# One more score block turned by DMA, with another table of steps, in a two-layer attention and token-mixer kernel

## The chip, the cores and the metric

The kernel runs on one core of a Trainium2 chip. The metric is the device time in microseconds of one execution, as the median of several. Before the change it is 765.40 us (three runs, 765.38 to 765.44). The core has TensorE (PE, with its weight loads shown as PEld), VectorE (DVE), ScalarE (ACT), GpSimd (POOL) and SyncE (SP), which here issues nearly all DMAs in one queue.

## The reference

There are two layers on 8 batches of 3200 rows. The first is an attention with a squared ReLU; its scores are z times its own transpose, so they are symmetric. The second mixes the tokens with weights that come from x itself.

```python
scores = (1.0 / S) * np.matmul(z, z.transpose(0, 2, 1))      # z: [8, 3200, 64]
attn = np.maximum(scores, 0.0) ** 2
x = u * np.matmul(attn, v)                                    # u, v: [8, 3200, 256]
wq, wk = x @ w_q, x @ w_k                                     # [8, 3200, 64]
W_tok = (1.0 / np.sqrt(64)) * np.einsum('bsd,btd->bst', wq, wk)
mixed = np.einsum('bst,btd->bsd', W_tok, x)
out = np.maximum(mixed, 0.0) @ w_out                          # w_out: [256, 256]
```

## The kernel before

**Tiles.** The 3200 rows of a batch are 25 row tiles of 128. As columns they make seven groups: groups 0 to 5 are 512 wide (four row tiles each), group 6 is 128 wide (one row tile). A score tile is one row tile against one group: 128 x 512, made by one matmul with 64 rows of contraction, so two of them run as a pair on the lower and the upper half of the array (`scores`, L296). The pair is emptied from PSUM into `g` by DVE or ACT with the ReLU (`first_stage`, L316 to L324), then squared by POOL or ACT into an fp16 tile `at` (`second_stage`, L326, L332 and L330). PSUM has three tiles for all of this (`pps`), and there are eleven `at` tiles.

**Turned blocks.** Scores are symmetric and so are their squares. A square whose block (gi, gj) is "turned" (`is_turned`, L237) is made once in group gi's columns, and a DMA transpose on SP's queue (L351) writes its mirror image into a home `tt`, from where it serves group gj. Block (gi, gj) means row group gj in group gi's columns. With `FAR = 2`, the blocks (0,1), (0,2), (1,2), (1,3), (2,3), (2,4), (3,4), (3,5), (4,5) are turned, and (0,4) besides: ten a batch, each of four score tiles, and two transposes each. There are seven homes (L285 to L294), given out by when the block in them was last read. Narrow mirror images for group 6 (`ts`) are turned as well.

**The second product.** For each group, x's 512 rows are the sum over all 25 row tiles of the transposed squares times v (`second_product`, L464). Its items are matmuls of 256 columns into two PSUM banks. Each is split into two with 64 rows of contraction, which run side by side: in the first pass the lower half works on one bank and the upper half on the other, then the lanes change banks (`swap_after`, L443) for the second pass. At the end of a group `gate` (L488) multiplies by u (DVE reads one bank at L507; ACT copies the other at L506 and POOL multiplies at L509). In the seventh group of a batch the two lanes keep one bank each (`is_split`).

**The second layer.** `turn_x` (L512) transposes x by DMA into one of four tiles. A "key block" (`keys_and_heads`, L813) projects x to queries and keys on TensorE, transposes the keys by DMA, and sums keys times x of the group before. When a batch is through, `mix` (L652) and `mix_out` (L678, on ACT) make the mixed rows for two groups at a time, and `project` (L804) multiplies a group of them by w_out, scales it on ACT (L739) and stores it.

**Steps.** The loop at L1028 runs in steps k = 3 to 167. A step scores up to six tiles (four if it holds a mix), empties them, squares those of the step before, and consumes, for the current group, tiles made two steps earlier (`LAG`) and turned tiles. How many steps a group gets follows from how many tiles are ready. A step may hold one key block, or one projection, or one mix, with or without a projection. Rules decide which (`key_due`, `mix_due`), except at the steps in the table `chosen` (L911), where letters say it: k, m, p. `heading_more` moves one score pair out of the head of a step. Loads, casts and transposes for the next batch are due a fixed number of steps after a batch began (`group_begun`, L866). After the loop a written order (`ENDING`) does what is left, with exactly three output groups still to be projected (`fillers`, L1237 and L1248).

Of the kernel before, what the change touches and what calls it, by code (L numbers as in the profile page):

```python
# [16 lines left out]
def kernel(  # L17
# [25 lines left out]
    FAR = 2  # L43
# [27 lines left out]
    def ps_tile(name):  # L71
        return pps.tile([P, 2, W], FP32, tag="ps", name=name)
# [162 lines left out]
    LASTG = NG - 1  # L235

    def is_turned(gi, gj):  # L237
        return gi < gj < LASTG and (gj <= gi + FAR or (gi, gj) == (0, 4))

# [2 lines left out]
    def group_of(ti):  # L244
        return max(gi for gi in range(NG) if starts[gi] <= ti * P)
# [8 lines left out]
    for b in range(B):  # L254
        for gi in range(NG):
            near = [t for t in range(NT) if is_turned(gi, group_of(t))]
            own = [
                t for t in range(NT) if t not in near and not is_turned(group_of(t), gi)
            ]
            if gi == LASTG:  # L260
                own = [t for t in own if group_of(t) not in FOR_SMALL]
            if b == 0 and gi == 0:
                order = [t for n0, nn in ZCH for t in range(n0, n0 + nn)]
                assert sorted(order) == sorted(near + own)
            else:
                odd = len(tiles) % 2
                order, rest = own[:odd], own[odd:]
                n_, m_ = len(near) // 2, (len(rest) + 1) // 2
                at_ = sorted(
                    [((i + 0.5) / max(n_, 1), near[2 * i : 2 * i + 2]) for i in range(n_)]  # L270
                    + [((i + 0.7) / max(m_, 1), rest[2 * i : 2 * i + 2]) for i in range(m_)]
                )
                for _, two in at_:
                    order = order + two
                if rest and len(rest) % 2:
                    order.remove(rest[-1])
                    order.append(rest[-1])
            many = W // widths[gi]
            tiles += [(b, gi, order[i : i + many]) for i in range(0, len(order), many)]
            ends[b, gi] = len(tiles)  # L280
# [5 lines left out]
    for b, gi, tis in tiles:  # L286
        gj = group_of(tis[0])
        if is_turned(gi, gj) and (b, gi, gj) not in tt_of:
            lefts = [t for t in range(NT) if is_turned(group_of(t), gj)]
            last_read = lefts.index(starts[gi] // P + 3) + 1  # L290
            tt_free.sort()
            tt_of[b, gi, gj] = tt_free[0][1]
            tt_free[0] = (b * NG + gj + last_read / len(lefts), tt_of[b, gi, gj])
# [79 lines left out]
    def whole(banks):  # L373
        return [
            lambda i=i: i.emit(ALL, i.start, i.stop) for bank in banks for i in bank
        ]
# [317 lines left out]
    def proj_items(b, gi, banks, half):  # L694
        js = range(2 * half, min(2 * half + 2, widths[gi] // P))
        return [
            Item(
                out=banks[half][:, ds((j % 2) * D, D)],
                lhsT=lambda r, dc=dc, j=j: rts[b, gi][r, dc, ts(j, P)],
                rhs=lambda r, dc=dc: wo[r, dc, :],  # L700
                start=(dc == 0 and j == js[0]),
                stop=(dc == ND - 1 and j == js[-1]),
            )
            for dc in range(ND)
            for j in js
        ]
# [14 lines left out]
    def proj_out(b, gi, src, ways):  # L721

        n0 = starts[gi] // P
        if groups:
            fo = pfo.tile([P, 2, W], FP32, tag="fo", name="fo")
        else:
            fo = pg.tile([P, 2, W], FP32, tag="g", name="fo")
        flat_out = fo[:].rearrange("p a w -> p (a w)")
        at = 0
        for on_dve, queue, n in ways:  # L730
            sl = slice(at * D, (at + n) * D)
            part = src[at // 2][:, 0 : n * D] if isinstance(src, list) else src[:, sl]
            if on_dve:
                nc.vector.tensor_scalar(
                    out=flat_out[:, sl], in0=part, scalar1=FINAL_SCALE, scalar2=None,
                    op0=AOP.mult,
                )
            else:
                nc.scalar.mul(out=flat_out[:, sl], in_=part, mul=FINAL_SCALE)  # L739
            queue.dma_start(  # L740
                out=rows(out, b)[:, n0 + at : n0 + at + n, :],
                in_=flat_out[:, sl].rearrange("p (n d) -> p n d", d=D),
            )
            at += n
# [41 lines left out]
    fillers = []  # L786
    to_load = []
    todo_mix, todo_proj, todo_between, at_phase, side = [], [], [], {}, []
# [15 lines left out]
    def project(b, gi):  # L804

        ps = ps_tile("fo")
        banks = [ps[:, 0, :], ps[:, 1, :]]
        src = ps[:].rearrange("p a w -> p (a w)")
        return [proj_items(b, gi, banks, half) for half in range(2)], lambda: proj_out(
            b, gi, src, [(False, nc.sync, widths[gi] // P)]  # L810
        )
# [54 lines left out]
    def group_begun(k, b, gi):  # L866
# [40 lines left out]

    heading_more = {165: -1}  # L910
    chosen = {  # L911
        18: "k", 19: "p", 20: "p", 21: "m", 35: "k", 36: "p", 38: "p", 101: "p", 142: "mp",
        147: "k", 148: "m", 149: "m", 159: "mp", 161: "p", 163: "m"
    }

    def mix_due(k):
# [104 lines left out]
    produced, consumed, k = 16, 6, 3  # L1021
# [6 lines left out]
    while groups:  # L1028
# [71 lines left out]
        b, gi = groups[0]  # L1100
# [134 lines left out]

    assert not at_phase and not side and not todo_between 
    fillers = todo_proj + fillers  # L1237
    assert not todo_mix and len(fillers) <= 3

    def acc_banks(name):  # L1240
        return [acc_tile(half, f"{name}{half}")[:] for half in range(2)]
# [112 lines left out]
```

## Time and profile before

| | |
|---|---|
| median of 3 runs | 765.40 us |
| the profiled execution | 765.49 us |
| its span, first to last instruction | 763.7 us |
| granted TensorE clock | 0.998 |
| TensorE busy | 754.3 us |
| ScalarE, GpSimd, VectorE busy | 551.1, 537.1, 461.9 us |
| busy share of the DMA queue of SP | 91.2% of 16 engines |
| HBM read, written | 59.38 MB, 26.21 MB |

All times are those of one profiled execution. A group's row names the line, the engine, the operation, what is written from what, the count, then the busy time, the mean of one in ns, and the idle time of the engine just before such instructions with what ended it. The chain is followed back from the last instruction: at each step to what released it. A matmul's duration is its latency; since matmuls overlap, the chain's pieces are the better measure of what a stretch costs. The DMA share adds up the times of packets, also of those that wait beside each other, so it can pass 1.

### The profile page before, as it was taken

How to read it: one execution, taken by the hardware profiler on the slowest of the kernel's cores; microseconds unless marked ns; L12 is line 12 of the kernel's file. 1: busy time of each engine (PE TensorE's matmuls, PEld its weight loads, DVE VectorE, ACT ScalarE, POOL GpSimd, SP SyncE). 2: the span in 40 equal slices, each digit the busy share in tenths (PEclk: the TensorE clock that was granted, in tenths of full speed). 3: DMA queues.
4: the chain of work that ended last, by engine and by line, in shares of the span. 5: the costliest groups of instructions: out<-in, count | busy, mean ns of one | idle time of the engine just before them, and what ended most of it. 6: DMA issues, size and time to landing. Idle time of an engine off the chain costs nothing.

```text
span 763.7 us, 29059 instructions
## 1 busy us (share of the span) xinstructions
PE 754.3 (99%) x12888; PEld 618.0 (81%) x12888; DVE 461.9 (60%) x458; ACT 551.1 (72%) x651; POOL 537.1 (70%) x351
## 2 busy tenths in 40 slices
PE   9999999999999999999999999999999999999996
PEld 6777888888888887888888888888878888888884
DVE  7655676546755567555665557656566565755534
ACT  8666776677767777687776877759777697776555
POOL 7897797768766678676787668866688665854540
PEclk9999999999999999999999999999999999999999
DMA  8999789887999969997899998999899999798636
GB/s 178 189 197 219 187 187 192 174 181 160 206 196 233 219 166 185 221 235 195 214 177 219 243 195 181 158 228 265 135 223 189 228 250 156 161 222 193 176 74 262
DMA packets 289614, 150.23 MB, mean 197 GB/s; under 512 B 265168, under 2 KB 268752, under 8 KB 289488
## 3 DMA queue, kind: packets, MB, share of 16 engines
q1 hardware_dynamic: 288768, 146.48, 91.2%
q0 software_dynamic: 576, 1.64, 1.1%
q8 instruction: 100, 1.64, 0.9%
q14 instruction: 26, 0.21, 0.1%
q10 hardware_dynamic: 144, 0.26, 0.1%
HBM read 59.38 MB, written 26.21 MB: 112 GB/s over the span
## 4 chain that ended last, share of the span: by engine, by line
PE 97%; DVE 2%; issue 0%; DMA 0%; ACT 0%; DVEq 0%; ACTq 0%
PE acc L369 72%; PE sc L307 12%; PE fo L369 5%; PE qk L369 5%; PE mx L657 1%; DVE x_sb L507 1%; DVE fo L1312 0%; DVE g L321 0%; PE ztp L130 0%; DMA z<-in_z_dram 0%; PE qk L610 0%; DVE zT L136 0%; PE xtx L634 0%; PE hd L644 0%; ACT fo L1316 0%
## 5 line engine op out<-in xcount | busy, mean ns | idle before, releaser
L321 DVE TENSOR_SCALAR g<-sc 128x1024 f32<-128x1024 f32 x329 | 400.5, 1223 | 240.5 <-PE sc L307 225.9
L332 POOL TENSOR_TENSOR at<-g 128x1024 f16<-128x1024 f32 x229 | 431.4, 1893 | 131.1 <-DVE g L321 106.5
L369 PE MATMUL acc<-v_sb,at 64*128 64x256 f16 (+1 forms) x7187 | 461.8, 269 | 1.6 <-DVE x_sb L507 0.5
L369 PEld LDWEIGHTS <-at 64*128 64x128 f16 (+1 forms) x7187 | 353.9, 94 | 86.9 <-PE acc L369 25.4
L330 ACT ACTIVATE at<-g 128x1024 f16<-128x1024 f32 x227 | 236.1, 1056 | 14.3 <-DVE g L321 7.2
L369 PE MATMUL acc<-v_sb,tt 64*128 64x256 f16 x2552 | 178.7, 269 | 0.0
L307 PE MATMUL sc<-zT 64*128 64x512 f16 (+1 forms) x1008 | 165.3, 357 | 0.2
L319 ACT ACTIVATE g<-sc 128x1024 f32<-128x1024 f32 x127 | 130.0, 1024 | 45.5 <-PE sc L307 43.2
L369 PEld LDWEIGHTS <-tt 64*128 64x128 f16 x2552 | 130.1, 94 | 14.2
L509 POOL TENSOR_TENSOR x_sb<-gt,u_sb 128x512 f16<-128x512 f32 x48 | 61.2, 1276 | 66.2 <-ACT gt L506 61.8
L678 ACT ACTIVATE rt<-mx 128x1024 f16<-128x1024 f32 x47 | 47.9, 1024 | 32.6 <-PE mx L657 32.5
L506 ACT COPY gt<-acc 128x512 f32<-128x512 f32 x48 | 28.0, 584 | 46.5 <-PE acc L369 44.7
L307 PEld LDWEIGHTS <-zT 64*128 64x128 f16 x1008 | 51.9, 94 | 8.8 <-issue 1.7
L369 PE MATMUL fo<-wo,rt 64*128 64x256 f16 (+1 forms) x696 | 57.9, 270 | 0.0
L544 ACT CAST qk<-qk 128x512 f16<-128x512 f32 x47 | 27.5, 585 | 34.3 <-PE qk L369 31.6
L369 PEld LDWEIGHTS <-rt 64*128 64x128 f16 (+1 forms) x696 | 35.5, 94 | 15.3 <-PE fo L369 6.3
L507 DVE TENSOR_TENSOR x_sb<-acc,u_sb 128x512 f16<-128x512 f32 x48 | 33.2, 691 | 20.3 <-PE acc L369 19.5
L739 ACT ACTIVATE fo<-fo 128x1024 f32<-128x1024 f32 x39 | 39.9, 1024 | 1.9 <-PE fo L369 1.7
L369 PEld LDWEIGHTS <-x_sb 64*128 64x128 f16 x672 | 29.8, 95 | 4.5 <-PE qk L369 0.9
L369 PE MATMUL qk<-kx,x_sb 64*128 64x64 f16 x672 | 32.8, 190 | 0.0
L369 PE MATMUL qk<-xT_sb,wkq 64*128 64x512 f16 (+3 forms) x118 | 25.8, 326 | 0.0
L369 PE MATMUL qk<-xT_sb,wqk 64*128 64x384 f16 (+3 forms) x148 | 24.8, 296 | 0.0
(86 smaller groups left out, 275.2 us busy)
## 6 DMA issues: line engine op xcount, KB each, us to landing
u_sb<-in_u_dram SPq DMA_DIRECT2D x48, 512.0 KB, 5.5
out_dram<-fo SPq DMA_DIRECT2D x43, 512.0 KB, 4.1
piece<-in_v_dram SPq DMA_DIRECT2D x42, 512.0 KB, 5.2
piece<-in_z_dram SPq DMA_DIRECT2D x7, 512.0 KB, 5.2
tt<-at SPq DMA_TRANSPOSE x162, 4.6
out_dram<-fo SPq DMA_DIRECT2D x9, 256.0 KB, 2.9
piece<-in_z_dram SPq DMA_DIRECT2D x7, 288.0 KB, 4.9
u_sb<-in_u_dram SPq DMA_DIRECT2D x8, 128.0 KB, 4.2
```

Source lines behind the costliest of these rows:

```text
L307: nc.tensor.matmul(out=sc[:, h, at : at + w], lhsT=zT[b][half : half + dqk, ds(z_at(b, h) + ti * P, P)], rhs=zT[b][half : half + dqk, ds(z ...
L319: nc.scalar.activation(out=g[:], in_=sc[:], func=RELU, scale=GSCALE)
L321: nc.vector.tensor_scalar(out=g[:], in0=sc[:], scalar1=0.0, scalar2=GSCALE, op0=AOP.max, op1=AOP.mult)
L330: nc.scalar.square(out=out, in_=g[:])
L332: nc.gpsimd.tensor_mul(out=out, in0=g[:], in1=g[:])
L369: return nc.tensor.matmul(out=self.out, lhsT=self.lhsT(rows), rhs=self.rhs(rows), start=start, stop=stop)
L506: nc.scalar.copy(out=upper[:], in_=accs[1][:])
L507: nc.vector.tensor_mul(out=x[:, 0:n], in0=accs[0][:, 0:n], in1=ug[:, 0:n])
L509: nc.gpsimd.tensor_mul(out=x[:, n : 2 * n], in0=upper[:], in1=ug[:, n : 2 * n])
L544: nc.scalar.copy(out=qks[b, gi][:, 0:gw], in_=out)
L678: nc.scalar.activation(out=out, in_=ps[:], func=RELU)
L739: nc.scalar.mul(out=flat_out[:, sl], in_=part, mul=FINAL_SCALE)
```

## The change

Row group 5 in group 2's columns becomes a turned block too: block (2,5). Its four tiles are squared in group 2 as before, and two more DMA transposes a batch write the mirror image for group 5. Group 5 computes 13 row tiles instead of 17 and reads 12 turned ones instead of 8. The number of score tiles falls from 912 to 880, and that of the steps by five (k = 3 to 162). The table of hand-chosen steps is another, since the steps have moved. The homes are the same seven, and they are given out anew by the same rule. In the last batch, the mixes that are left when scoring is over are three instead of two, and four output groups instead of three are left after the loop; the new lines project the first of them there, before the written ending.

```diff
     def is_turned(gi, gj):
-        return gi < gj < LASTG and (gj <= gi + FAR or (gi, gj) == (0, 4))
+        return gi < gj < LASTG and (gj <= gi + FAR or (gi, gj) in ((0, 4), (2, 5)))
...
-    heading_more = {165: -1}
+    heading_more = {64: -1}
     chosen = {
-        18: "k", 19: "p", 20: "p", 21: "m", 35: "k", 36: "p", 38: "p", 101: "p", 142: "mp",
-        147: "k", 148: "m", 149: "m", 159: "mp", 161: "p", 163: "m"
+        16: "m", 40: "k", 41: "p", 59: "", 139: "p", 140: "m", 141: "m", 142: "p", 143: "m",
+        145: "p"
     }
...
     fillers = todo_proj + fillers
-    assert not todo_mix and len(fillers) <= 3
+    assert not todo_mix
+    while len(fillers) > 3:
+        made_now, done_now = project(*fillers.pop(0))
+        for fn in whole(made_now):
+            fn()
+        done_now()
```

## The prediction

> **What bounds the kernel now.** I read the page's shares and chain first, then eight equal stretches of the span, then the chain inside single steps. The page:
>
> ```profile
> span 763.7 us, 29059 instructions
> PE 754.3 (99%) x12888; PEld 618.0 (81%) x12888; DVE 461.9 (60%) x458; ACT 551.1 (72%) x651; POOL 537.1 (70%) x351
> PE 97%; DVE 2%; issue 0%; DMA 0%; ACT 0%; DVEq 0%; ACTq 0%
> L321 DVE TENSOR_SCALAR g<-sc 128x1024 f32<-128x1024 f32 x329 | 400.5, 1223 | 240.5 <-PE sc L307 225.9
> L332 POOL TENSOR_TENSOR at<-g 128x1024 f16<-128x1024 f32 x229 | 431.4, 1893 | 131.1 <-DVE g L321 106.5
> L369 PE MATMUL acc<-v_sb,at 64*128 64x256 f16 (+1 forms) x7187 | 461.8, 269 | 1.6 <-DVE x_sb L507 0.5
> L330 ACT ACTIVATE at<-g 128x1024 f16<-128x1024 f32 x227 | 236.1, 1056 | 14.3 <-DVE g L321 7.2
> L319 ACT ACTIVATE g<-sc 128x1024 f32<-128x1024 f32 x127 | 130.0, 1024 | 45.5 <-PE sc L307 43.2
> ```
>
> TensorE is the chain (97%), and the 7187 product matmuls idled before them for 1.6 us in all. The other engines wait for it: DVE stood 225.9 us until a score matmul ended. By stretches (us, busy time of PE, PEld, DVE, ACT, POOL, then clock, DMA share, GB/s):
>
> ```profile
> 95.50:190.90 95.40, 95.13 (x1671) 79.33 (x1667) 57.69 (x58) 68.92 (x83) 75.32 (x48) 1.00 0.86 179
> 477.30:572.80 95.50, 95.37 (x1680) 78.54 (x1678) 58.88 (x57) 70.88 (x84) 69.81 (x44) 1.00 1.00 202
> ```
>
> PE leaves 0.13 us of 95.5 idle at full clock, so time is matmul columns. The DMA share stands at 1.00, which makes DMA the second thing to watch. It is a sum over packets and no saturation: a single step shows 1.24 and PE stays whole there (3.29 of 3.29):
>
> ```profile
> 102.17:105.46 3.29, 3.29 (x58) 2.55 (x54) 2.38 (x3) 2.65 (x3) 3.29 (x3) 1.00 1.24 269
> ```
>
> The chain inside a plain step (start, us, what) gives the prices:
>
> ```profile
> 99.04 0.43 PE sc L307 x4
> 99.48 1.31 PE acc L369 x24
> 100.79 0.22 PE sc L307 x2
> 101.00 1.33 PE acc L369 x24
> ```
>
> Two score matmuls run side by side on the two halves of the array, so a pair of them is 0.43/2 = 0.215 us, and 24 product matmuls take 1.31 us. The step is nothing else.
>
> **The change, part by part.**
>
> *Scores.* Block (2,5) gets its transpose from a DMA, so block (5,2) is no longer computed: 4 tiles a batch, 32 in all, 880 - 32 = 848 wide score matmuls, 16 pairs. 16 x 0.215 = 3.4 us leave the chain. The Trainium skill (TensorE: Matmul & The Clock Gate, Back-to-back issue gap) gives about 131 ns a matmul of 512 columns in a stream; 32 of them would be an estimated 4.2 us, and the sum below would end 0.8 us lower. The trace disagrees (0.43 us for four), because two share the array.
>
> *Evictions and squares.* 16 pairs fewer: by the built order DVE 329 to 318 and ACT 127 to 122 first stages, POOL 229 to 219 and ACT 227 to 221 squares. 11 x 1.223 = 13.5 us of DVE, 10 x 1.893 = 18.9 us of POOL, 5 x 1.024 + 6 x 1.056 = 11.5 us of ACT. These lie beside PE and are worth 0.
>
> *Steps.* The step loop runs to 162 instead of 167, since six tiles are scored a step and group 5 now takes two steps, not three. The product's items stay 5000. The two lanes change banks 232 instead of 239 times. What such a change costs:
>
> ```profile
> PEld L369 <- PE acc L369: 25.4, 106, 0.3
> ```
>
> A weight load waits 25.4/106 = 0.24 us there, but in the plain step above the score pair of 100.79 stands in the gap and the pass after it takes 1.33 against 1.31. So between 0.02 and 0.24 each, 0.1 to 1.7 us for seven; I take 0.2, by the step, which is PE itself.
>
> *Group starts.* At a group's start PE needs the accumulators that DVE and ACT are reading, and runs scores meanwhile. With a projection or a key block in the step the wait is covered; without one it isn't:
>
> ```profile
> 163.50 0.66 PE sc L307 x12
> 164.17 2.28 PE acc L369 x36
> 166.49 2.14 PE acc L369 x35
> ...
> 212.12 0.46 PE fo L369 x8
> 212.58 1.97 PE acc L369 x36
> 214.76 1.99 PE acc L369 x35
> ...
> 181.41 0.65 PE sc L307 x6
> 182.06 1.64 PE acc L369 x28
> 183.75 1.70 PE acc L369 x27
> ...
> 163.57 0.69 DVE L507 TENSOR_TENSOR x_sb<-acc,u_sb 128x512 f16<-128x512 f32 x1 [1.37 <-PE acc L369]
> ```
>
> At 163.50 three score pairs (0.66) are shorter than the DVE read that ends at 163.57 + 0.69 = 164.26, and the two passes take (2.28 - 1.97) + (2.14 - 1.99) = 0.46 us more than those at 212.58, which a projection covers. After the narrow seventh group (181.41) it is 1.64 + 1.70 against 55/24 x 1.31 = 3.00, so 0.3. By the step tables the start is bare at steps 7, 10, 37 (wide) and 41, 104 (narrow) before; after, at 7, 10, 16, 34, 44 (wide) and 141 (narrow, a mix and two score pairs). Net 2 x 0.46 - 0.3 = +0.6 us.
>
> *Moved key blocks and mixes.* Steps 79, 99 (a key block) and 140 (a mix) now share the step of a seventh group, which held a projection or nothing before. No row shows it: at best it covers the start as a projection does (0), at worst it costs a bare start, 0.46 each. I take 0, as the key block is the same kind of TensorE work as the projection.
>
> *The end.* Three mixes instead of two are flushed when scoring is over (step 160), and one output group, (6, 2), is projected after the loop. The matmul columns are the same. Each flushed mix is emptied by ACT:
>
> ```profile
> L678 ACT ACTIVATE rt<-mx 128x1024 f16<-128x1024 f32 x47 | 47.9, 1024 | 32.6 <-PE mx L657 32.5
> ...
> ACT G L1269 <- PE xtx L634: 3.9, 1, 3.9
> ```
>
> With three PSUM tiles the third mix needs one that a score eviction has left; the last pair is emitted half a step earlier, so 0, at worst one ACT row, 1.0 us. The later scaling of (6, 2), 1.0 us on ACT, falls into the 3.9 us that ACT stands before G: 0. Without that cover G would start up to 1.0 later. I take 0.1 for both.
>
> *DMA.* 16 more transposes, two a batch, go on SP's queue while group 2's columns are made; nothing leaves that queue. On SP and to landing:
>
> ```profile
> L351 SPq DMA_TRANSPOSE tt<-at x162: 1195/1373/4432, 13.1 to 719.6; - x162
> DMA to landing us min/median/max: 2.5/4.6/9.7
> SPq L351 <- POOL at L332: 45.9, 34, 3.0
> ACT at L330 <- DMA tt<-at: 4.8, 2, 3.2
> POOL at L332 <- DMA out_dram<-fo: 2.3, 1, 2.3
> ```
>
> 16 x 1.373 = 22 us of SP. Behind them in the queue stand x's transposes, the key transposes, u, the next batch's v and z, and the stores. The seven homes of turned blocks now hold eleven blocks a batch, not ten: by the tables a home is written in the very step of its last reader three times (steps 50, 91, 110) and in the step after it 17 times (twice before), and the transpose of x for (1, 5), asked for in step 39, waits for the key block of step 40, which frees the fourth of its tiles. Each holds SP for up to a step. The first reader of a turned block comes no sooner than two steps after its writing, as before. So PE need not notice: between 0 and the 4.8 + 2.3 us that ACT and POOL lost to DMAs in this trace. I take 0.2, near the low end, because PE lost nothing to those two.
>
> *Sum.* -3.4 - 0.2 + 0.6 + 0.1 + 0.2 = -2.7 us. The profiled execution took 765.49 us (span 763.7), 0.09 over the median of 765.40: 762.8 profiled, 762.7 as a median. Ends: -3.4 - 1.7 gives 760.4; the upper ends 0.6 + 1.4 + 1.0 + 7.1 on -3.5 give +6.6, 772.
>
> **The rivals.** (a) *The gain is eaten at the starts.* Key blocks and mix on the seventh group's steps cost a bare start each (3 x 0.46) and the third mix its 1.0: 762.7 + 2.4 = 765.1, no change. For it: the bare starts show that PE has no reserve at a group's start. Against: with a projection in that step the seventh group runs in this trace without a named wait.
>
> (b) *Slower: late transposes hold the `at` buffers.* Eleven at buffers feed PE; a square may not overwrite one whose transpose has not read it. The row "ACT at <- DMA tt" shows it twice, up to 3.2 us. In a plain step ACT has 3.29 us for a PSUM tile whose eviction takes 1.024, so some 2.3 us can be lost before PE waits. One wait of 3.2 a batch would cost 0.9 x 8 = 7.2: 769.9. It decides when PE loses over 2.7 + 1.5 = 4.2 us, 0.5 a batch. For: DMA share near 1.00 all through the middle, homes with no step to spare. Against: two such waits in 763.7 us now, and fewer squares.
>
> (c) *SP's issue is the bound.* If the sequencer that issues the DMAs set the pace, each of the 16 would lengthen the run: +22 us, 787. SP waits 45.9 us for POOL's squares alone, so it has time over. That a track solid with DMA issues is itself a bound is a rule of the Trainium skill (Perfetto Trace Analysis, What "DMA-bound" means); by that rule this trace is not there.
>
> **How the numbers follow.** Forecast 762.7, own range 761.0 to 763.8: 0.55. (a) 0.22. (b) 0.20. (c) 0.03. A measurement tells about 0.2%, 1.5 us, from no change: below 763.9 faster 0.55, up to 766.9 same 0.22, above it slower 0.23. The range reaches from 761.0 up to 767.5, where (a) and the weak cases of (b) lie; beyond it I leave 0.14, below it 0.04.
>
> **What the profile after would show.** Scores: 976 rows of L307 instead of 1008, its share of the chain down by 0.4 points. Starts: passes of 2.2 to 2.3 us for 36 matmuls at steps 16, 34, 44. DMA: tt<-at +16, landing times longer in the middle, more SP waits for PE. (a) shows as PE idle before acc at the seventh groups and at the flush. (b) shows as "ACT at" or "POOL at" waiting for DMA tt<-at many times, and then PE idle before sc. I am wrong if PE's idle time before L307 and L369, 1.8 us together with the next row, grows by more than 4 us.
>
> ```profile
> L307 PE MATMUL sc<-zT 64*128 64x512 f16 (+1 forms) x1008 | 165.3, 357 | 0.2
> ```

## The result and the profile after

The changed kernel takes 770.87 us as a median (767.31 to 773.31), the kernel before beside it 765.42 (765.38 to 765.76). The ratio is 1.0065, with a 95% interval from 1.0046 to 1.0084: slower by 0.65%, where 762.7 us had been forecast. The profiled execution of the changed kernel, 767.31 us, is the fastest of its four, so its trace shows the least of the loss. The four lie 6 us apart; those of the kernel before lie 0.4 us apart here, and 0.8 to 5.2 us in the larger sets further down.

The page of the changed kernel, the lines that answer to those shown of before:

```profile
span 765.4 us, 28908 instructions
PE 751.6 (98%) x12820; PEld 618.5 (81%) x12820; DVE 446.9 (58%) x447; ACT 541.7 (71%) x641; POOL 517.7 (68%) x340
q1 hardware_dynamic: 305664, 150.67, 95.3%
PE 92%; DMA 2%; DVE 2%; ACT 1%; issue 1%; POOL 0%; ACTq 0%; DVEq 0%; POOLq 0%
L332 POOL TENSOR_TENSOR at<-g 128x1024 f16<-128x1024 f32 x219 | 412.3, 1894 | 126.0 <-DVE g L321 71.9
L369 PE MATMUL acc<-v_sb,at 64*128 64x256 f16 (+1 forms) x6931 | 448.8, 269 | 2.3 <-DMA v_sb<-in_v_dram 0.9
L330 ACT ACTIVATE at<-g 128x1024 f16<-128x1024 f32 x221 | 229.4, 1055 | 36.0 <-DMA tt<-at 23.0
L307 PE MATMUL sc<-zT 64*128 64x512 f16 (+1 forms) x976 | 160.5, 356 | 1.0 <-ACT g L319 0.6
L369 PE MATMUL qk<-kx,x_sb 64*128 64x64 f16 x672 | 32.8, 190 | 1.1 <-DMA kx<-qk 1.1
```

TensorE has less work and is the chain for 92% of the span instead of 97%. DMAs, 0% before, now carry 2% of it. ACT's idle time before its squares has grown from 14.3 to 36.0 us, and most of it (23.0) ends with the landing of `tt`. The waits of the changed kernel (us in all, times, longest) say the same of POOL:

```profile
POOL at L332 <- DMA tt<-at: 28.3, 11, 3.7
ACT at L330 <- DMA tt<-at: 23.0, 9, 4.9
POOL v_sb L151 <- DMA piece<-in_v_dram: 8.1, 4, 4.1
```

Before, ACT's row was 4.8 us in two waits, and the two others did not exist. Two of the 95 us stretches, with the columns of the prediction's windows:

```profile
477.30:572.80 95.50, 95.37 (x1688) 78.95 (x1686) 56.57 (x57) 69.17 (x83) 66.68 (x42) 1.00 1.01 215
572.80:668.20 95.40, 94.10 (x1670) 78.40 (x1668) 57.01 (x56) 71.28 (x84) 65.48 (x42) 1.00 1.07 209
```

One of them is as whole as before (0.13 us idle), the next has lost 1.3 us. The loss sits at single places.

**What is late.** The landing time of `tt` has hardly moved (median 4.7 us, 4.6 before). It is the issue that comes late. The DMA queue of SP in the changed kernel (start, us, what):

```profile
152.53 1.35 SPq L351 DMA_TRANSPOSE tt<-at  x1
153.97 1.22 SPq L351 DMA_TRANSPOSE ts<-at  x1
155.28 1.20 SPq L551 DMA_TRANSPOSE kx<-qk  x1
156.57 1.18 SPq L551 DMA_TRANSPOSE kx<-ql  x1
157.80 0.57 SPq L195 DMA_DIRECT2D u_sb<-in_u_dram  x1
158.47 2.15 SPq L351 DMA_TRANSPOSE tt<-at  x1
```

There is no room between them. The key transpose at 156.57 belongs to step 32, whose first matmul stands at 137.20:

```profile
137.20 0.59 PE L307 MATMUL sc<-zT 64*128 64x512 f16 x4
```

So it is issued 19.4 us after its step began. SP issues in the order in which the code asks, so this lateness (issue of a DMA less the first matmul of the step that asks for it) can be worked out for each DMA of the step loop. It counts from the step's start, so a DMA that the step asks for late has some us even in an idle queue; what tells is the comparison. Its median, 90th percentile and largest value are 6.0, 9.5 and 12.4 us before, and 8.2, 13.9 and 19.4 after. The longest stretch in which SP issues one DMA right behind another (under 0.3 us between them) grows from 67 us (47 DMAs) to 82 us (58 DMAs, from 94 us on).

**Where TensorE waits.** A step's loss is its length less what its matmuls cost at the rate of the plain step. The sum of the losses has grown by 5.1 us, and 3.4 us of scores are gone; the difference is the 1.7 us by which the spans differ. Of the 5.1 us, 0.6 stand in the opening (in this profile alone; two later ones of the same kernel do not have them), 1.0 in the ending, and most of the rest at steps 16, 18, 95 and 146. At step 146 the chain names the DMA:

```profile
658.72 4.25 DMA kx<-qk
662.97 0.05 issue
663.02 0.52 PE qk L369 x10
```

Step 146 multiplies x by the keys of step 144, whose transpose was issued at 658.72, two short steps earlier. Ahead of steps 16, 18 and 95 the path is the one of rival (b). ACT before step 95, which begins at 425.85:

```profile
421.97 1.06 ACT L330 ACTIVATE at<-g 128x1024 f16<-128x1024 f32 x1 [3.01 <-DMA tt<-at]
...
425.81 1.00 ACT L319 ACTIVATE g<-sc 128x1024 f32<-128x1024 f32 x1
```

A square waits 3.01 us for its `at` buffer, what stands behind it on ACT is late, the eviction at 425.81 too, and TensorE, which needs that PSUM tile, loses 1.0 us.

### The profile page after: what moved, and what is told of

Its sections match the earlier page's. It is cut to its first block, busy times and chain, and to the rows that moved or that the text cites. A ratio compares the mean times of both kernels' runs of the same rounds, so it can differ in the third digit from the quotient of the medians.

```text
span 765.4 us, 28908 instructions
## 1 busy us (share of the span) xinstructions
PE 751.6 (98%) x12820; PEld 618.5 (81%) x12820; DVE 446.9 (58%) x447; ACT 541.7 (71%) x641; POOL 517.7 (68%) x340
## 4 chain that ended last, share of the span: by engine, by line
PE 92%; DMA 2%; DVE 2%; ACT 1%; issue 1%; POOL 0%; ACTq 0%; DVEq 0%; POOLq 0%
PE acc L369 69%; PE sc L307 11%; PE fo L369 5%; PE qk L369 5%; PE mx L657 1%; DVE g L321 1%; DMA v_sb<-in_v_dram 1%; DMA tt<-at 1%; DMA kx<-qk 1%; DVE x_sb L507 1%; ACT g L319 0%; DVE fo L1317 0%; ACT at L330 0%; ACT zT L188 0%; POOL at L332 0%
## 5 line engine op out<-in xcount | busy, mean ns | idle before, releaser
L321 DVE TENSOR_SCALAR g<-sc 128x1024 f32<-128x1024 f32 x318 | 386.5, 1223 | 238.9 <-PE sc L307 232.8
L332 POOL TENSOR_TENSOR at<-g 128x1024 f16<-128x1024 f32 x219 | 412.3, 1894 | 126.0 <-DVE g L321 71.9
L369 PE MATMUL acc<-v_sb,at 64*128 64x256 f16 (+1 forms) x6931 | 448.8, 269 | 2.3 <-DMA v_sb<-in_v_dram 0.9
L369 PEld LDWEIGHTS <-at 64*128 64x128 f16 (+1 forms) x6931 | 345.0, 94 | 82.6 <-PE acc L369 24.5
L330 ACT ACTIVATE at<-g 128x1024 f16<-128x1024 f32 x221 | 229.4, 1055 | 36.0 <-DMA tt<-at 23.0
L369 PE MATMUL acc<-v_sb,tt 64*128 64x256 f16 (+1 forms) x2776 | 189.1, 269 | 0.0
L307 PE MATMUL sc<-zT 64*128 64x512 f16 (+1 forms) x976 | 160.5, 356 | 1.0 <-ACT g L319 0.6
L369 PEld LDWEIGHTS <-tt 64*128 64x128 f16 (+1 forms) x2776 | 140.9, 94 | 15.3
L319 ACT ACTIVATE g<-sc 128x1024 f32<-128x1024 f32 x122 | 124.6, 1021 | 34.9 <-PE sc L307 33.5
L151 POOL CAST v_sb<-piece 128x1024 f16<-128x1024 f32 (+1 forms) x23 | 22.6, 981 | 8.1 <-DMA piece<-in_v_dram 8.1
```

The costliest lines, as they stand in the source:

```text
L307: nc.tensor.matmul(out=sc[:, h, at : at + w], lhsT=zT[b][half : half + dqk, ds(z_at(b, h) + ti * P, P)], rhs=zT[b][half : half + dqk, ds(z ...
L319: nc.scalar.activation(out=g[:], in_=sc[:], func=RELU, scale=GSCALE)
L321: nc.vector.tensor_scalar(out=g[:], in0=sc[:], scalar1=0.0, scalar2=GSCALE, op0=AOP.max, op1=AOP.mult)
L330: nc.scalar.square(out=out, in_=g[:])
L332: nc.gpsimd.tensor_mul(out=out, in0=g[:], in1=g[:])
L369: return nc.tensor.matmul(out=self.out, lhsT=self.lhsT(rows), rhs=self.rhs(rows), start=start, stop=stop)
```

## The experiments

Three theories were put to test. **Q**: SP's queue falls behind through its time for issuing, and what waits for it reaches TensorE. **D**: the transfers of the 16 transposes are the cost, through the DMA engines. **T**: the step table (bare starts, moved key blocks and mixes) is the cost. Medians are in us; each is to be read beside the kernel before in the same set of runs, which took 765.4 to 765.9.

### The 16 transposes taken out

Block (2,4)'s home is kept until group 5 has read it, too.

```diff
...
+            if (gi, gj) == (2, 5):
+                turned[b, gi, gj] = turned[b, 2, 4]
+                continue
```

> The changed kernel without the 16 transposes of block (2,5): block (5,2) reads the turned block (2,4) in its place, so the output of that block is left out. TensorE's work and the step table are those of the changed kernel, SP issues as many transposes as before. If the loss comes from the added transposes on SP's queue (theory Q) or from DMA traffic (theory D), the gain of the scores is seen: 762.5 to 764.0 us, and the longest time that an issue on SP comes after its step's start falls back from 19.4 to about 12.5 us. If the loss comes from the new step table, the bare starts and the moved key blocks and mixes (theory T), it stays at 769 to 771.

Measured 764.41 (763.62 to 766.22), ratio 0.9984 (0.9972 to 0.9997); lateness 11.3 us at the 90th percentile, 17.3 at most where about 12.5 had been expected. So part of the scores' gain is there, the transposes eat it and more, and T is not the main cause. But only 1.4 us are gained (1.9 in the profiled execution, 0.5 of them after the last matmul), not 2.9. The losses up to the last matmul tell where: 1.9 us more than before, of which 1.0 stands in the ending. The chain there in the kernel before:

```profile
744.02 0.44 PE fo L369 x4
744.46 0.44 PE hd L369 x4
```

and in this run:

```profile
740.65 0.89 PE fo L378 x8
741.54 0.02 issue
741.56 0.02 ACTq L748
741.58 0.04 issue
741.62 1.03 ACT fo L748
742.65 0.04 issue
742.69 0.60 PE hd L378 x4
```

The scaling of the output group that is now projected after the loop (1.03 us on ACT) stands on the chain, since `hd` needs the PSUM tile that it empties. The other 0.9 us are the bare starts at steps 16, 34 and 44 (0.64 to 0.69 lost in each, lane change included) and step 150, less those that went.

### The same transposes in the kernel before

```diff
...
-            if is_turned(gi, gj) or (gj == LASTG and gi in FOR_SMALL):
+            if is_turned(gi, gj) or (gi, gj) == (2, 5) or (gj == LASTG and gi in FOR_SMALL):
```

The homes are given out as in the changed kernel.

> The kernel before, with its step table and all its scores, plus the 16 transposes of block (2,5), which nothing reads; the block takes its home among the seven as long as in the changed kernel. Theory Q: the loss without the gain, 765.4 plus up to 8 us: 768 to 774, POOL and ACT waiting for DMA tt<-at for 20 us and more. Theory D: the same sign. Theory T: 765.2 to 766.0.

Measured 766.07 (764.89 to 769.53), ratio 1.001 (0.9999 to 1.0022), a miss for Q and D: nearly no loss, though SP is as late as in the changed kernel (13.6 at the 90th percentile) and POOL and ACT wait 33.8 and 12.3 us for `tt`. So the transposes cost little in the table of steps of before. That TensorE has less reserve against them in the changed kernel's shorter table fits this, and a later run with the transposes unread (below), but what in the table takes the reserve was not tested.

### Stores moved to ACT's queue

```diff
-            b, gi, src, [(False, nc.sync, widths[gi] // P)]
+            b, gi, src, [(False, nc.scalar, widths[gi] // P)]
```

> The changed kernel with the 45 or so stores of the step loop issued from ACT's queue instead of SP's; about 0.56 us each, some 25 us, leave SP, as much as the transposes of (2,5) added, and the DMA traffic is the same. Theory Q (SP's in-order queue falls behind): 762.5 to 764.5 us. Theory D (the transfers themselves, a DMA share of 1.01 to 1.07): no change, 769 to 771. Theory T (step table): no change, 769 to 771, or more, as ACT carries the issues.

> The kernel before with the same stores on ACT's queue, the control. Theory Q: SP was not the limit before, 765.0 to 765.8. If ACT's issue work costs PE anything by itself, it shows here: over 766.

Measured 780.91 with the change and 775.19 without it, where 763 and 765 had been expected of Q. The control shows why this says nothing on Q. ACT's timeline in the kernel before with that edit:

```profile
414.19 1.02 ACT L739 ACTIVATE fo<-fo 128x1024 f32<-128x1024 f32 x1
418.40 0.34 ACTq L740 DMA_DIRECT2D out_dram<-fo  x1
418.85 1.06 ACT L330 ACTIVATE at<-g 128x1024 f16<-128x1024 f32 x1 [3.63 <-DMA tt<-at]
```

The store stood for 3.2 us before it was issued. In the trace all DMAs of SP and ACT share eight completion semaphores in turn, and the store's was that of a transpose which SP had issued late:

```profile
412.75 1.24 SPq L351 DMA_TRANSPOSE tt<-at  x1
```

That one landed 5.6 us later, at 418.33, when ACT went on. So SP's lateness was passed on to ACT.

### The changed kernel again, and with the transposes unread

> The changed kernel once more, beside the three others on the same chip: 769 to 772 us if its loss of 5.4 us is its own and not that of one chip. Theory Q (SP's in-order queue falls behind, and what waits for it on POOL, ACT and PE stands at places that change from execution to execution) expects a spread of several us, and in the profile of a slower execution PE's idle time at more steps than 16, 95 and 146.

In the next kernel block (5,2) reads block (2,4)'s mirror image, and that of (2,5) is made for nobody; the homes are given out to suit:

```diff
...
-        return turned[b, gj, gi][rows, j, ti - starts[gj] // P, :]
+        read = 4 if (gj, gi) == (2, 5) else gi
+        return turned[b, gj, read][rows, j, ti - starts[gj] // P, :]
```

> The changed kernel with all its transposes, of which those of block (2,5) are read by nothing: block (5,2) reads the turned block (2,4), and the home of (2,5) comes free soon after its writing. The output of that block is left out. Theory Q: the 16 transposes cost the same whether they are read or not, 769 to 771 us, as the changed kernel. Theory H (the reads hold the homes and the homes hold SP): as without the transposes, 764 to 765.5.

Measured 771.95 (766.91 to 776.62), ratio 1.0088 (1.006 to 1.0117), for the first, and 766.88 (765.03 to 772.65), ratio 1.003 (1.0014 to 1.0046), for the second. The loss is the change's own. With the unread transposes the kernel is 1.5 us above the kernel before of its set, without them it was 1.4 below: they cost some 3 us, the read ones more. Neither Q's 769 to 771 nor H's 764 to 765.5 was met. Homes that hold SP (theory H) are not the reason: where SP is more than 6 us late, it stands still for only some 10 us in all in the changed kernel, 7.6 of them once, at step 39. What the reading adds stayed open; a later set of the changed kernel took only 768.47.

### Stores left out, and stores cut to a quarter

The first edit leaves out the store while the step loop runs, the second stores one row tile of four:

```diff
-                out=rows(out, b)[:, n0 + at : n0 + at + n, :],
-                in_=flat_out[:, sl].rearrange("p (n d) -> p n d", d=D),
+                out=rows(out, b)[:, n0 + at : n0 + at + (1 if groups else n), :],
+                in_=flat_out[:, ds(at * D, (1 if groups else n) * D)].rearrange("p (n d) -> p n d", d=D),
```

> The changed kernel without the stores of the step loop (their part of the output is left out): 43 issues of about 0.56 us, 24 us, leave SP, and 20 MB of traffic with them. Theory Q and theory D (the transfers) both: 762.5 to 764.5. If it stays at 769 or more, neither the queue nor the traffic is the cause, and the dependence of (5,2) on the turned block is.

> The changed kernel with the same stores of the step loop cut to a quarter of their bytes (three quarters of their output are left out): SP issues as many DMAs as the changed kernel, the engines move some 15 MB less. Theory Q: 768 to 771, as the changed kernel. Theory D: most of the gain of leaving the stores out, 763 to 765.

Measured 763.94 (ratio 0.9982, 0.9974 to 0.9991) without the stores and 764.78 (0.9988, 0.998 to 0.9997) with a quarter of their bytes. With as many issues on SP the loss is gone, as D had it. With a quarter of the bytes the lateness hardly falls (13.6 at the 90th percentile; 12.0 without the stores), and the transfers land a little sooner (4.36 us in the mean for all transposes, 4.54 in the changed kernel of the same set). But SP's issuing gets shorter as well, 621 us in all instead of 642, nearly all of it on the transposes, so this run alone does not part D from Q. The kernel before was not run without its stores, so what part of the gain belongs to the change is open.

### A twelfth at buffer, and a key block one step earlier

The room comes from one `qk` tile and one of the two `rs` tiles (the edit of `rs` is not shown).

```diff
-    NAT = 11
+    NAT = 12
...
-    pq = ctx.enter_context(tc.tile_pool(name="pq", bufs=11))
+    pq = ctx.enter_context(tc.tile_pool(name="pq", bufs=10))
...
-        16: "m", 40: "k", 41: "p", 59: "", 139: "p", 140: "m", 141: "m", 142: "p", 143: "m",
-        145: "p"
+        16: "m", 40: "k", 41: "p", 59: "", 139: "p", 140: "m", 141: "m", 142: "p", 143: "k",
+        144: "m", 145: "p"
```

> The changed kernel with twelve at buffers instead of eleven; their room comes from one qk tile (ten instead of eleven) and one of the two rs tiles. Transposes, traffic and step table are those of the changed kernel. Theory B (transposes that SP issues late hold the at buffers, squares on POOL and ACT wait, then TensorE): POOL and ACT wait for DMA tt<-at for under 20 us instead of 40 to 50, and the time falls to 764 to 767 us. If the lateness acts through the key transposes and v's pieces instead, it stays at 769 to 772.

> The changed kernel with the key block of step 144 one step earlier, so that three steps lie between it and the next one, at step 146, which reads its turned keys; the mix of step 143 moves to 144. If TensorE's wait for DMA kx<-qk at step 146 (1.4 to 1.5 us in two profiles) and the lower clock that follows a longer wait are a main part of the loss: 766 to 769 us. If they are a small part: 769 to 771.

> Both edits together, with the 16 transposes and the whole traffic kept. Theory B with the wait at step 146: 762.7 to 764.5 us, the sum of the prediction without its DMA term, below the kernel before. If neither is the cause: 769 to 772.

Measured 766.51 (763.67 to 770.85, ratio 1.0013, 0.9997 to 1.003), 768.08 (ratio 1.0035, 1.0017 to 1.0052) and 767.76 (ratio 1.0024, 1.001 to 1.0038). The changed kernel in the same set took 768.47 (ratio 1.005). So the twelfth buffer is worth some 2 us, just clear of the spread, the key block nothing that can be told; and beside the earlier key block the buffer is worth 0.3, which is not clear. Both together had been expected at 762.7 to 764.5 by the theory of held buffers, a miss of 3 us. The waits with twelve buffers:

```profile
POOL v_sb L151 <- DMA piece<-in_v_dram: 15.2, 5, 7.1
POOL at L332 <- DMA tt<-at: 11.9, 7, 2.8
ACT at L330 <- DMA tt<-at: 5.4, 5, 3.0
```

The squares wait 17 us instead of 40 to 51, and v's pieces, next in the same late queue, take over: 15.2 instead of 8.1.

### A slower execution

> The changed kernel once more, for another profile of it. If the spread of its executions (767 to 777 us) comes from TensorE waiting longer at the same few steps, and from a clock granted at half after such a wait, a profile of a slower execution shows steps 52, 95 and 146 with losses of 2 us and more and the granted clock near 0.5 behind them.

This run's own profile is of a faster execution again (768.16 us); the losses at steps 16, 95, 137 and 146 are 0.8 to 1.4 us, and the clock stays at 1.00. But the profile with the earlier key block is of an execution of 771.21 us. Its chain at step 52, and its windows there:

```profile
229.12 5.66 DMA tt<-at
...
234.86 0.04 ACT at L330
...
235.82 1.01 ACT g L319
236.84 0.04 issue
236.88 0.42 PE mx L657 x2
```

```profile
233.00:235.00 2.00, 1.58 (x30) 1.26 (x25) 0.41 (x1) 0.14 (x1) 0.00 (x0) 1.00 0.83 184
235.00:237.00 2.00, 0.12 (x2) 0.11 (x3) 0.00 (x0) 2.00 (x3) 1.26 (x1) 1.00 0.94 258
237.00:239.00 2.00, 2.00 (x19) 1.45 (x17) 0.55 (x2) 1.98 (x4) 2.00 (x2) 0.53 1.22 248
239.00:241.00 2.00, 2.00 (x24) 1.56 (x22) 0.87 (x1) 1.98 (x3) 1.47 (x2) 0.62 0.92 151
```

This is rival (b) at work: a transpose issued late lands at 234.78, the square that waited for its buffer starts, then the eviction, then TensorE, which has stood for 2.3 us. And then its granted clock is 0.53 and 0.62 for the next 4 us: step 52 loses 2.6 us, and step 53, which waits for nothing, 1.8 more.

### Loads of u on POOL's queue, and small issues in place of the transposes

```diff
-        nc.sync.dma_start(out=us[b, gi][:, 0:nn, :]
+        nc.gpsimd.dma_start(out=us[b, gi][:, 0:nn, :]
```

> The changed kernel with the 56 loads of u issued from POOL's queue: some 35 us of issuing leave SP (56 x 0.63), as many as the 16 transposes and more put on it, and the traffic is the same. POOL issues the first loads of v in 0.53 us each, so it gets about 30 us on 518. If SP's time for issuing is the cause (theory Q): 763 to 765.5. If the traffic is (theory D): 768 to 772.

> The kernel before with the same loads on POOL's queue, the control. Theory Q: PE loses almost nothing to SP there, 765.0 to 765.8. Over 766.5: the issues on POOL cost by themselves, and the run beside it is to be read by its distance to this one.

> The changed kernel with twelve at buffers and the loads of u on POOL's queue. If late transposes and their hold on the at buffers are the whole loss: 762.5 to 764, the sum of the prediction without its DMA term. If something else is left: over 765.

The small issues stand where the transposes stood, and block (5,2) again reads block (2,4)'s mirror image:

```diff
...
+            if (gi, gj) == (2, 5):
+                turned[b, gi, gj] = turned[b, 2, 4]
+                for i in range(3):
+                    turns.append(
+                        lambda i=3 * (n0 // 2) + i: nc.sync.dma_start(
+                            out=tiny[i][:], in_=rows(u, 0)[:, 0, 0:4]
+                        )
+                    )
+                continue
```

> The changed kernel without the 16 transposes (block (5,2) reads the turned block (2,4), the output of that block is left out), and with 48 loads of 16 bytes a partition put on SP's queue at the same places, three for each transpose: about 20 to 26 us of issuing without traffic to speak of, in place of the transposes' 23. Theory Q: 767 to 771, as the changed kernel. Theory D: 764 to 765, as without the transposes.

Measured 776.81 (ratio 1.0121) with the change, 770.55 (1.0055) without it, 781.33 (1.0185) with the twelfth buffer, and 764.62 (0.9995, 0.9981 to 1.0009) with the small issues. Nothing was relieved by moving u: the control loses 5.1 us, the change still costs 6.3 on top, SP's lateness is 15.4 us at the 90th percentile, and the transposes land later (min, median, max; 2.4, 4.7 and 8.6 in the changed kernel):

```profile
DMA to landing us min/median/max: 3.0/5.2/11.9
```

That agrees with a rule of the Trainium skill (DMA: Bandwidth & Descriptors, Issuing engines are not separate DMA queues): DMAs run on the same sixteen engines whoever starts them, and another issuer saves only the issuing. Here that saving bought less than it cost. In the control's profile a single transpose took 11.2 us to land, the square that needed its buffer waited, and TensorE lost 5.3 us in that one step (26): a slow transfer reaches TensorE by the same path as a late issue.

The small issues are the clean half. SP's issuing adds up to 635 us (608 without the transposes, 639 to 642 in the changed kernel), its lateness is the changed kernel's (13.8 and 19.4 us at the 90th percentile and the most), and so are the waits:

```profile
POOL at L339 <- DMA tt<-at: 25.5, 11, 5.2
ACT at L337 <- DMA tt<-at: 13.9, 7, 4.4
```

Yet the time is that without the transposes. So Q falls as the sole cause: issues that hold no square and move few bytes do no harm that can be told. And the waits of POOL and ACT alone do not set the time either, since they are as long here as in the changed kernel.

### v's pieces three steps earlier

```diff
-    V_LATER = [(7, 5), (9, 4), (11, 4), (13, 3), (14, 3), (15, 3), (17, 4)]
+    V_LATER = [(4, 5), (6, 4), (8, 4), (10, 3), (11, 3), (12, 3), (14, 4)]
```

> The changed kernel with the loads of v and their casts three steps earlier in each batch (from the fourth to the fourteenth step of a batch instead of the seventh to the seventeenth), in the stretch where SP comes 5 to 7 us late instead of 10 to 14. If the held at buffers are the larger part: 766 to 769, POOL's wait for v's pieces under 3 us, the waits for DMA tt<-at 30 us or more. If v's pieces are the larger part: 764 to 766.

> Twelve at buffers and the loads of v three steps earlier. If held at buffers and late pieces of v are the whole loss: 763.3 to 764.8 us, as the kernel without the 16 transposes, and below the kernel before. If something else is left: 766 and more.

Measured 784.77 (ratio 1.0246, 1.0224 to 1.0268) and 786.99 (1.0269, 1.024 to 1.0298), a miss of 20 us. The same DMAs, asked for at other steps, make SP later than ever (17.4 at the 90th percentile, 23.0 at most). The waits of the first:

```profile
POOL at L332 <- DMA tt<-at: 58.9, 18, 6.8
ACT at L330 <- DMA tt<-at: 41.2, 16, 7.9
POOL v_sb L151 <- DMA piece<-in_v_dram: 14.3, 6, 4.3
```

Steps 52, 53, 95, 114 and 115 lose 1.8 to 7.1 us each, and the mean clock is 0.987. It was no remedy, but it shows how steep the loss can be: with the step table and DMA count unchanged, the kernel with 3.4 us more lateness takes 13 to 16 us longer. With twelve buffers the squares wait 26.2 us instead of 100.1, v's pieces 42.1 (POOL and ACT) instead of 21.8, and the time is no better. So the `at` buffers are not the only way by which a late DMA reaches TensorE.

### What the runs say together

Lateness and waits (of the squares on POOL and ACT for `tt`) are each from one profile, which need not be of a median execution; the first four kernels have the table of steps of before, the others the changed one:

| | lateness, 90th percentile | squares waiting for tt | median |
|---|---|---|---|
| before | 9.5 | 4.8 | 765.4 |
| before, stores on ACT's queue | 9.5 | 24.0 | 775.2 |
| before, u on POOL's queue | 11.1 | 12.9 | 770.6 |
| before, with the 16 transposes | 13.6 | 46.1 | 766.1 |
| without the 16 transposes | 11.3 | 17.7 | 764.4 |
| without the stores | 12.0 | 34.8 | 763.9 |
| stores' bytes a quarter | 13.6 | 41.5 | 764.8 |
| small issues instead | 13.8 | 39.4 | 764.6 |
| transposes unread | 14.3 | 54.5 | 766.9 |
| twelve at buffers | 14.4 | 17.3 | 766.5 |
| changed kernel | 13.9 to 14.3 | 40 to 51 | 768.5 to 772.0 |
| u on POOL's queue | 15.4 | 80.3 | 776.8 |
| v earlier | 17.4 | 100.1 | 784.8 |
| v earlier, twelve at buffers | 17.3 | 26.2 | 787.0 |

Neither column gives the time: at a lateness of 13.6 to 14.4 us it lies between 764.6 and 772.0, and the kernel before with its stores or its loads of u moved is at 775.2 and 770.6 with less. What is shown is that the 16 transposes in the changed table of steps make the loss, that SP's time for issuing does not make it alone, and that it goes when the transposes or the stores' bytes go; one more buffer takes away about half of it in one set, and nothing that can be told beside the earlier key block. That the changed kernel stands at an edge, past which late transfers reach TensorE and now and then cost it its clock, fits its spread and the run with v earlier, but no run shows the edge itself. Whether the 16 transposes do it by the bytes that they move or by the squares that they hold could not be told apart: no run had the one without the other. No kernel that computes everything beat the kernel before.

## Why the prediction was wrong

**Scores.** Right: 976 rows, and 3.4 us of matmul columns less. **Evictions and squares** beside PE: right, and they brought nothing. **Steps and starts**: the bare starts came at steps 16, 34 and 44 with 0.64 to 0.69 us lost in each, as in such steps before (0.65 at steps 10 and 37); moved key blocks and the mix on steps 79, 99 and 140 cost nothing beyond what a split step cost before (0.36 to 0.41), as taken. No run isolates the 0.2 for the seven lane changes. Rival (a) is not what happened.

**The end.** Mis-sized: 0.1 was taken, 1.0 measured. The cover named was ACT's 3.9 us ahead of `G`; the work did fall into it, but TensorE needed the PSUM tile that the scaling empties, which I had asked of the flushed mixes only.

**DMA.** The step that failed. It ended with "so PE need not notice: between 0 and the 4.8 + 2.3 us", and took 0.2. Against the run without the transposes it is 4.5 to 8.0 us, each kernel taken by its distance from the kernel before of its own set. Two readings led there. The first is that landing times and named waits of the trace of before were taken as the price of 16 more transposes. The median landing time has hardly moved, and the waits did not stay what they were: 4.8 us became 40 to 51. What could have been read before is how late SP is at its issues and how long it goes on without a pause, 47 DMAs in 67 us. That is a warning and not a price, since the small issues left the lateness and took the loss away. The second is that SP's 45.9 us of waiting were called time to spare. They lie elsewhere in the batch than those stretches, and a queue in order can't use them.

The sign that was named for being wrong did not show. TensorE's idle time before its scores and products grew from 1.8 to 3.3 us in the profile, not by more than 4: the profile is of the fastest execution, only 1.8 us above that of the kernel before, and in slower ones matmuls at a lower clock count as busy (2.00 of 2.00 us at 0.53, above).

**The rivals.** (b) had the mechanism, `at` buffers held by late transposes, the direction, and with 769.9 nearly the time, at a chance of 0.20. Its sign stood in the text: ACT's wait for `tt` did rise from 2 times to 9, and POOL's to 11. It did not have the clock, which turns a wait of 2.3 us into a loss of 4.4, nor the pieces of v and the key transposes that stand in the same queue. (c) is refuted: 16 transposes did not cost SP's 22 us, and the small issues with 24.6 us on SP cost nothing that can be told. The range ended at 767.5, as if (b) came only in weak cases. That its 769.9 lies near the measured 770.9 is in part luck: it counted one wait a batch, where the losses stand at a few steps and change from execution to execution.

## What to carry to other kernels

Before adding a DMA to an in-order queue, work out how late that queue already is (issue less the time at which the code asks for it) and how long it runs without a pause; the landing time of single transfers and the mean busy share hide it. When buffers are held until a transfer has read them, their number sets how late a transfer may be, and several late things in one queue can make the loss past that steep. Here a change took 0.5% of the work from TensorE and put 4% more issuing on the queue that feeds it, and the second weighed more.

## What was not expected of the hardware

A short wait can cost TensorE twice. After 2.3 us without matmuls within 4 us, its granted clock stood at 0.53 and 0.62 for the next 4 us (above), and in the run with the unread transposes in the kernel before 1.8 us of idleness sufficed: step 57 lost 2.0 us and step 58, at a clock of 0.51 to 0.64, another 2.4. Waits of 1.0 to 1.4 us (steps 95 and 146) left the clock at 1.00. The Trainium skill (TensorE: Matmul & The Clock Gate, Part 1: The HAM clock gate) states that the clock halves after an idle window of some 3.4 us and comes back after as long a busy one. The length of the slow stretch agrees: if the clock was either full or half, 0.53 and 0.62 over two windows of 2 us are an estimated 3.4 us at half. The idle time that suffices was shorter here.

Moving plain loads or stores to another engine's queue made both kernels slower, the kernel before by 5.1 us (u on POOL) and 9.3 (stores on ACT), though those engines were busy for 70% and 72% only.
